# Matmuls of the K and V tiles as register-addressed loops, and a new split of the last weight rows

## The chip, the cores and the metric

The kernel runs on one core of one Trainium2 chip, in a single launch. The metric is device time in microseconds (us) of the whole program; the figure for a kernel is the median of its runs. Five engines work side by side and each runs its own instruction list in order: TensorE (PE in the profile; its weight loads are listed apart as PEld), VectorE (DVE), ScalarE (ACT), GpSimd (POOL) and SyncE (SP), which here only issues transfers. Transfers are carried out by 16 DMA engines. Engines and transfers wait for one another through semaphores.

## The reference, cut to what matters

One decode step: attention of one token over a cache of 65,536 keys and values for 8 heads of 256 (two query heads share each), a small gated feed-forward block, and a sigmoid gate that mixes the two.

```python
B, Sq, D = 1, 1, 448
Hq, Hkv, Sk, Dh = 16, 8, 65536, 256          # F = 1792, all bf16
g = _sigmoid((x * gate_w).sum(-1, keepdims=True))
# a:
q = (x @ wq).reshape(B, Sq, Hq, Dh).transpose(0, 2, 1, 3)
scores = jnp.einsum("bhqd,bhkd->bhqk", q, k) * (Dh ** -0.5)
o = jnp.einsum("bhqk,bhkd->bhqd", softmax(scores), v)
a = o.transpose(0, 2, 1, 3).reshape(B, Sq, Hq * Dh) @ wo
# b:
gate = x @ W_gate; up = x @ W_up
h = gate * (gate > 0) * up
b = h @ W_down
return g * a + (1 - g) * b
```

K and V are 268 MB each; all other inputs together are about 12 MB.

## The kernel before

**Tiles.** K and V are read in tiles of 16,384 positions of one head, each 128 partitions x 32768 bf16 (8.39 MB): 32 K tiles and 32 V tiles, four of each per head. They lie in a ring of three buffers, `ring[0]` to `ring[2]`. Every load of a tile goes out on SP's queue, in the order of the list `order`: the projection weights, K tiles 0 to 3, then V and K in turn, at the end V tiles 28 and 29, part of Wo, V tile 30, V tile 31 in three pieces and the rest of Wo. A load may be issued only when the matmuls that read the buffer's earlier tile are done (`free`, semaphore waits on SP). SP issues in order, so a load that waits holds back all behind it. `TILE = 19.35` is the time that the plan allows for a tile.

**K tile** (`kind == "k"`). VectorE transposes the tile in place in 32x32 blocks of 32-bit words (L379; the first four tiles in two halves, all others in one piece). Then TensorE computes scores (`f_qk`, 64 matmuls of 512 columns): the queries `xm` are the weights (16 columns), the transposed tile streams. Results go to two PSUM tiles `ST0` and `ST1`, each to four strips of 32 partitions. The strip is the matmul's `tile_position=(0, 32 * w)`, one of four column strips of TensorE's array that can work at the same time. The second matmul of a strip uses the weights that the first one loaded (`same_weights`, which leaves the weight load out). VectorE then joins the halves (L594) and takes the maximum (L596), ScalarE takes the exponential (L598). After the fourth K tile of a head a short chain over VectorE, TensorE and ScalarE scales the head's probabilities, which are then transposed (L604 to L624).

**V tile** (`make_pv`). TensorE multiplies probabilities `P0` or `P1` (32 weight columns) with the V tile, 128 matmuls of 512 columns to the four PSUM tiles `O0` to `O3` and four strips each. After a head's fourth V tile VectorE, TensorE and ScalarE collect the result (`o_copy`, `f_otr`, `f_nrm`). The last V tile comes in pieces, with small fill-in matmuls (`f_busy`) between them.

**Order.** The kernel lists operations with a key, the planned time (`op`, `dma`); `_Plan.finish` sorts each engine's operations by key and derives the semaphore waits; `emit` writes them out and lets the last instruction of each operation raise its engine's semaphore by one. The order on TensorE around a steady pair of tiles is: QK of a K tile, then PV of the V tile that has landed.

**Feed-forward rows.** 448 input rows are 3 x 128 + 64. The 64 rows left over of W_gate and W_up are loaded by `rows64` (L402 to L408) into `wfh`, in four transfers per matrix: 5 partitions with 4 rows each, again 5 with 4, 5 with 3, and 3 with 3, interleaved (partition `c + 4 i` of transfer `c`). `f_xp` (L307) lays the matching 64 entries of x out in the same pattern, and `f_gu2` (L556) multiplies them, over 20 partitions and four blocks; places without a row are zero.

Of the kernel before, what the change touches and what calls it, by code (L numbers as in the profile page):

```python
# [1 line left out]

# [13 lines left out]
class _Op:  # L16


    def __init__(self, eng, key, fn, deps, dma=None):
        self.eng, self.key, self.fn, self.dma = eng, key, fn, dma  # L20
        self.deps = [d for d in deps if d is not None]
        self.count = None


class _Plan:
# [8 lines left out]
    def op(self, eng, key, fn, deps=()):  # L34
        o = _Op(eng, key, fn, deps)
        self.ops.append(o)
        return o

# [14 lines left out]
    def finish(self):  # L53
        progs = {}
        for i, o in enumerate(self.ops):
            o.seq = i
            for d in o.deps:
                assert (d.key, d.seq if hasattr(d, "seq") else -1) <= (o.key, i), (o.eng, o.key, d.eng, d.key)
        for e in ("sp", "pe", "dv", "ac", "gp"):
            progs[e] = sorted((o for o in self.ops if o.eng == e), key=lambda o: (o.key, o.seq))  # L60
        ndma = {}
        for e, prog in progs.items():
            n = 0
            for o in prog:
# [12 lines left out]
        for o in sorted(self.ops, key=lambda o: (o.key, o.seq)):  # L77
            need, after = {}, {}
            for d in o.deps:
                k = ("d", d.dma) if d.dma is not None else ("e", d.eng)  # L80
                need[k] = max(need.get(k, 0), d.count)
                merge(after.setdefault(k, {}), d.known)
            o.waits = []
            for k, v in need.items():
                if past[o.eng].get(k, 0) < v and all(a.get(k, 0) < v for j, a in after.items() if j != k):
                    o.waits.append((k, v))
            merge(past[o.eng], need)
            for a in after.values():
                merge(past[o.eng], a)
            o.known = dict(past[o.eng])  # L90
        return progs
# [12 lines left out]
def bass_gated_mix__gqa_block_cached__glu_gated_reglu__decode_kernel(  # L104
# [23 lines left out]
    NT = H * NTH  # L128
# [11 lines left out]
    KR = D - NR3  # L140
# [3 lines left out]
    with es:  # L144
# [29 lines left out]
        xw = P2[0][:, 0:NW * 160]  # L174
# [132 lines left out]
        def f_xp(e):  # L307
            xr = x_row[0:1, NR3:D]
            for c in range(2):
                e.tensor_copy(x_per[0:1, 129 * c:129 * c + 127:2], xr)  # L310
            xp2 = x_per[0:1, 256:768].rearrange("o (b g p) -> o g b p", b=4, g=4)
            def two(v, b):
                return v.rearrange("o (i b) -> o b i", b=b).unsqueeze(1).to_broadcast([1, 2, b, v.shape[1] // b])
            for c in range(2):
                e.tensor_copy(xp2[:, 0:2, :, c:20:4], two(xr[:, 20 * c:20 * c + 20], 4))
            e.tensor_copy(xp2[:, 0:2, 0:3, 2:20:4], two(xr[:, 40:55], 3))
            return e.tensor_copy(xp2[:, 0:2, 0:3, 3:12:4], two(xr[:, 55:KR], 3))
        x0_ = op("dv", 0.5, f_xp, [d_x, c_xp])
        x1_ = mop("pe", 0.6, f_xT, [d_x, c_o1, x0_])

# [55 lines left out]
        def f_trans(sl, w, nw):  # L376
            m = U * DH // nw
            v = ring[sl][:, w * m:(w + 1) * m].bitcast(U32)
            return lambda e: e.transpose(v, v)  # L379

        def f_qk(n, sl):
            h = n // NTH
            kv = ring[sl][:].rearrange("p (u s c w j two) -> p s c w u j two", s=2, c=4, w=4, j=8, two=2)

            def f(e):
                for c in range(4):
                    for r_ in range(2):
                        x0 = ((h * 4 + c) * 2 + r_) * 16
                        for s_ in range(2):
                            for w in range(4):  # L390
                                o, v = ST[s_][32 * w:32 * w + 16, :], kv[:, s_, c, w, :, :, r_]
                                st = c == 0 and r_ == 0
                                if s_ == 0:
                                    ins = e.matmul(o, xm[:, x0:x0 + 16], v, start=st, stop=False, skip_group_check=True, tile_position=(0, 32 * w))  # L394
                                else:
                                    ins = same_weights(e, o, xm[:, x0:x0 + 16], v, st, (0, 32 * w))
# [76 lines left out]
        def make_pv(n, lo, hi, sl, tv, dep):  # L473
# [4 lines left out]
            def f_pv(e):  # L478
                for m in range(lo // 2, hi // 2):
                    I, i, g = m // 16, m // 4 % 4, m % 4  # L480
                    k = m if solo else I * 16 + g * 4 + i
                    b, n_ = (0, 4) if solo else (i, 32)
                    col = (k - b) * 32 + a
                    o, w = OP[b][32 * g:32 * g + n_, :], P2[h % 2][:, col:col + 4 * n_ - 3:4]
                    v = ring[sl][:, k * 512:(k + 1) * 512]
                    st = a == 0 and I == 0
                    if b == 0:
                        ins = e.matmul(o, w, v, start=st, stop=False, skip_group_check=True, tile_position=(0, 32 * g))  # L488
# [34 lines left out]
        for kind, i, t in issue:  # L523
# [59 lines left out]
            elif kind == "k":  # L583
# [10 lines left out]
                join = op("dv", tk + 25.2, lambda e: e.copy_predicated(  # L594
# [142 lines left out]
```

## Time and profile before

| | |
|---|---|
| median of 3 runs | 1277.44 us (1277.27 to 1277.6) |
| span of the profiled execution, first to last instruction | 1275.9 us |
| TensorE busy (matmul) | 353.7 us, 28% |
| VectorE busy | 683.4 us, 54% |
| ScalarE busy | 56.1 us, 4% |
| moved by DMA | 549.46 MB, mean 431 GB/s |

The profile is of one execution. Its span leaves out what lies around the program's first and last instruction, some 1.5 us against the median of the runs. A row of instructions gives the engine, the source line, the operation, what is written and read, the count, and, in brackets, how long the engine sat idle before it and whom it waited for. `SPq` rows are transfers being issued. Transfers have a time from issue to landing; what exceeds the pure transfer time was spent in the queue behind earlier ones. In a table of stretches each engine's busy time is followed by TensorE's granted clock (1.00 is full speed), the mean busy share of the 16 DMA engines, and GB/s.

### The profile page before, as it was taken

The numbers are of one execution on the slowest core, as the hardware profiler recorded it, in microseconds if no ns is written. First come the engines' busy times: TensorE is split into PE (matmuls) and PEld (weight loads), VectorE is DVE, ScalarE is ACT, GpSimd is POOL, SyncE is SP. The second block draws the span as 40 slices with busy tenths as digits, with TensorE's granted clock in tenths as the row PEclk, the third lists the DMA queues.
The fourth block names the chain that finished last, engine by engine and source line by source line (L and its number), as shares of the span: only waits on it lengthen the run. The fifth ranks groups of instructions, "written<-read, shape, count | busy, mean of one in ns | idle before, by whom it ended". The sixth has DMA issues, their size and how long they took to land.

```text
span 1275.9 us, 6860 instructions
## 1 busy us (share of the span) xinstructions
PE 353.7 (28%) x4446; PEld 71.6 (6%) x1875; DVE 683.4 (54%) x271; ACT 56.1 (4%) x104; POOL 10.6 (1%) x23
## 2 busy tenths in 40 slices
PE   3312323313122240133220242211323203322135
PEld 2000000000000000000000000000000000000010
DVE  2688733566534755445555454556535566336521
ACT  0000000000000000000000000000000000000000
POOL 3000000000000000000000000000000000000000
PEclk9566666665666565666755666656666556666577
DMA  9999999999999999999999999999999999999998
GB/s 407 433 436 434 438 428 429 442 427 436 431 426 448 429 428 434 430 434 438 428 434 438 430 434 428 432 438 438 428 428 436 436 438 428 428 438 436 434 417 372
DMA packets 11178, 549.46 MB, mean 431 GB/s; under 512 B 1255, under 2 KB 1386, under 8 KB 2154
## 3 DMA queue, kind: packets, MB, share of 16 engines
q1 hardware_dynamic: 11002, 547.66, 99.3%
q10 hardware_dynamic: 148, 1.38, 0.3%
q8 instruction: 24, 0.39, 0.1%
q14 instruction: 4, 0.03, 0.0%
HBM read 549.03 MB, written 0.00 MB: 430 GB/s over the span
## 4 chain that ended last, share of the span: by engine, by line
DVE 40%; DMA 28%; PE 17%; another core or an unknown queue 12%; ACT 1%; issue 1%; SPq 0%; ACTq 0%; DVEq 0%
DVE ring L379 32%; DMA ring<-in_A_k_cache_dram 24%; PE ST L394 5%; PE ST L420 5%; PE O L420 4%; DMA ring<-in_A_wo_dram 3%; DVE o_sb L429 2%; PE O L488 2%; DVE P L617 1%; DVE P L615 1%; ACT P L598 1%; DMA P<-in_A_x_dram 1%; DVE nmb L596 1%; DVE ST L594 1%
## 5 line engine op out<-in xcount | busy, mean ns | idle before, releaser
L379 DVE STREAM_TRANSPOSE ring<-ring 128x16384 uint32<-128x16384 uint32 (+1 forms) x36 | 552.3, 15345 | 315.9 <-DMA ring<-in_A_k_cache_dram 311.5
L394 PE MATMUL ST<-ring,xm 128*16 128x512 bf16 x1024 | 139.7, 537 | 769.2 <-DVE ring L379 769.2
L420 PE MATMUL ST<-ring,xm 128*16 128x512 bf16 x1024 | 136.7, 526 | 0.0
L420 PE MATMUL O<-ring,P 128*32 128x512 bf16 x1524 | 119.3, 425 | 0.0
L594 DVE COPY_PREDICATED ST<-bm,ST 128x512 f32<-128x512 uint16 x32 | 22.2, 693 | 169.3 <-PE ST L420 169.3
L598 ACT ACTIVATE P<-ST,nmb 128x512 bf16<-128x512 f32 x32 | 45.3, 1415 | 1099.3 <-DVE nmb L596 1099.3
L394 PEld LDWEIGHTS ST<-ring,xm 128*16 128x16 bf16 x1024 | 31.8, 115 | 925.8 <-DVE ring L379 797.9
L488 PE MATMUL O<-ring,P 128*32 128x512 bf16 (+1 forms) x524 | 56.7, 430 | 21.9 <-DMA ring<-in_A_v_cache_dram 21.9
L429 DVE CAST_PREDICATED o_sb<-bm,O 128x512 bf16<-128x512 uint16 (+1 forms) x33 | 22.3, 679 | 62.0 <-PE O L420 58.9
L615 DVE TENSOR_TENSOR P<-P,hs 128x2048 bf16<-128x2048 bf16 x8 | 18.3, 2292 | 8.7 <-ACT hs L612 8.7
L596 DVE TENSOR_REDUCE nmb<-ST 128x1 f32<-128x512 f32 x32 | 22.1, 691 | 1.1
L488 PEld LDWEIGHTS O<-ring,P 128*32 128x32 bf16 (+1 forms) x524 | 15.8, 114 | 119.3 <-issue 92.0
L617 DVE STREAM_TRANSPOSE P<-P 128x2048 bf16<-128x2048 bf16 x8 | 18.5, 2312 | 0.3
L622 PE MATMUL M_ps<-hs,ones_f 128*128 128x2 f32 x16 | 4.7, 363 | 46.0 <-DVE hs L621 46.0
L457 PE MATMUL M_ps<-emat,o_sb 128*64 128x2 bf16 x48 | 3.0, 184 | 22.1 <-ACT o_sb L439 22.1
L598 ACT ACTIVATION_READ_ACCUMULATOR P<-ST,nmb 128x1 f32 x32 | 8.5, 266 | 0.0
L345 PE MATMUL M_ps<-ring,P 128*128 128x256 bf16 x48 | 7.4, 330 | 0.3 <-DVE gb L297 0.3
L310 DVE COPY xm<-P 1x64 bf16<-1x64 bf16 x2 | 0.3, 189 | 11.9 <-DMA P<-in_A_x_dram 11.9
L622 PEld LDWEIGHTS M_ps<-hs,ones_f 128*128 128x128 f32 x16 | 4.0, 311 | 46.7 <-DVE hs L621 46.7
L608 PE MATMUL M_ps<-identf,hs 128*2 128x128 f32 x8 | 2.2, 277 | 15.7 <-DVE hs L606 15.7
L259 POOL MEMSET ring<- 64x7168 bf16 x1 | 6.1, 6064 | 0.3 <-POOLq L722 0.3
L345 PEld LDWEIGHTS M_ps<-ring,P 128*128 128x128 bf16 x48 | 5.6, 118 | 2.0 <-issue 0.4
(96 smaller groups left out, 82.6 us busy)
## 6 DMA issues: line engine op xcount, KB each, us to landing
ring<-in_A_v_cache_dram SPq DMA_DIRECT2D x1, 4096.0 KB, 29.6
ring<-in_A_v_cache_dram SPq DMA_DIRECT2D x2, 2048.0 KB, 36.0
ring<-in_A_wq_dram SPq DMA_DIRECT2D x1, 3072.0 KB, 13.3
ring<-in_A_wo_dram SPq DMA_DIRECT2D x1, 1792.0 KB, 19.4
ring<-in_B_W_down_dram SPq DMA_DIRECT2D x1, 1568.0 KB, 17.2
ring<-in_B_W_gate_dram ACTq DMA_DIRECT2D x1, 1344.0 KB, 13.1
ring<-in_B_W_up_dram SPq DMA_DIRECT2D x1, 1344.0 KB, 15.9
ring<-in_A_wo_dram SPq DMA_DIRECT2D x1, 896.0 KB, 40.0
```

Source lines behind the costliest of these rows:

```text
L345: ins = e.matmul(QN_ps, xw3[:, kt, 31 - j:159 - j], wq3[:, kt * NQ + j * 256:kt * NQ + (j + 1) * 256], start=(j == 0 and kt == 0), stop=Fa ...
L379: return lambda e: e.transpose(v, v)
L394: ins = e.matmul(o, xm[:, x0:x0 + 16], v, start=st, stop=False, skip_group_check=True, tile_position=(0, 32 * w))
L420: return e.add_instruction(mybir.InstMatmult(name=nc.get_next_instruction_name(), engine=e.engine, ins=[e.lower_ap(v), e.lower_ap(w, for_m ...
L429: return e.copy_predicated(dst, m.to_broadcast(list(src.shape)), src)
L488: ins = e.matmul(o, w, v, start=st, stop=False, skip_group_check=True, tile_position=(0, 32 * g))
L594: join = op("dv", tk + 25.2, lambda e: e.copy_predicated(ST[0][:], bm[:, NB:NB + 1].bitcast(mybir.dt.uint16).to_broadcast([128, 512]), ST[ ...
L596: smax[n] = op("dv", tk + 26, lambda e, n=n, NM=NM, t_=t_: e.tensor_reduce(NM[:, t_:t_ + 1], ST[0][:], AX.X, ALU.max, negate=True), [join, ...
L598: aexp[n] = op("ac", tk + 27, lambda e, n=n, t_=t_, NM=NM, RS=RS, Ph=Ph: e.activation(Ph[:, t_:2048:4], ST[0][:], ACTF.Exp, bias=NM[:, t_: ...
L615: rsc = op("dv", T + 16, lambda e, X=X, pb=pb: e.tensor_tensor(pb, pb, X[:, 12:16].unsqueeze(1).to_broadcast([128, 512, 4]), ALU.mult), [h ...
L617: last["ev", h] = [op("dv", T + 17, lambda e, Ph=Ph: e.transpose(Ph[:], Ph[:]), [rsc])]
L622: l3 = mop("pe", T + 19, lambda e, X=X: e.matmul(LS_ps, ones_f[:, :], X[:, 6:8], start=True, stop=True), [l2, c_one])
```

## The change

Two edits.

1. **Loops on TensorE.** `f_qk` writes out its first eight matmuls and then runs the other 56 as a loop of seven passes with eight matmuls. `f_pv` does the same for the V tiles 0 to 30 with 16 matmuls a pass: three passes after 16 written-out matmuls for a head's first V tile, four passes and nothing written out for the others. The last V tile stays as it was. Weight and data addresses are computed from the loop counter in TensorE's registers (`moved`, `raw_mm`). The last matmul of each pass raises the semaphore, so an operation now counts 7, 4 or 3 (`incs`). Inside a QK pass, and among the eight written out, the two matmuls that share a strip now follow each other.

2. **The 64 rows.** The four transfers per matrix now take 5 partitions with 4 rows three times, and 4 partitions with one row; `f_xp` follows.

```diff
@@ _Op, _Plan
-                    n += 1
+                    n += o.incs
@@ f_xp
-            for c in range(2):
+            for c in range(3):
                 e.tensor_copy(xp2[:, 0:2, :, c:20:4], two(xr[:, 20 * c:20 * c + 20], 4))
-            e.tensor_copy(xp2[:, 0:2, 0:3, 2:20:4], two(xr[:, 40:55], 3))
-            return e.tensor_copy(xp2[:, 0:2, 0:3, 3:12:4], two(xr[:, 55:KR], 3))
+            return e.tensor_copy(xp2[:, 0:2, 0:1, 3:16:4], two(xr[:, 60:KR], 1))
@@ f_qk
+        def moved(ap, by):
+            return dataclasses.replace(ap, offset=ap.offset + by)
+
+        def raw_mm(e, o, w, v, pos, load):
+            return e.add_instruction(mybir.InstMatmult(
+                name=nc.get_next_instruction_name(), engine=e.engine, ins=[v, w], outs=[e.lower_ap(o)],
+                start_tensor_calc=False, stop_tensor_calc=False, tile_size=(128, 32), tile_position=pos,
+                bass_skip_group_check=True, ldweights=None if load else False))
...
-                for c in range(4):
-                    for r_ in range(2):
-                        x0 = ((h * 4 + c) * 2 + r_) * 16
+                x0 = h * 8 * 16
+                for w in range(4):
+                    for s_ in range(2):
+                        o, v = ST[s_][32 * w:32 * w + 16, :], kv[:, s_, 0, w, :, :, 0]
+                        if s_ == 0:
+                            e.matmul(o, xm[:, x0:x0 + 16], v, start=True, stop=False, skip_group_check=True, tile_position=(0, 32 * w))
+                        else:
+                            same_weights(e, o, xm[:, x0:x0 + 16], v, True, (0, 32 * w))
+                with e.Fori(1, 8, 1) as k:
+                    by = (k >> 1) * 64 + (k & 1)
+                    xw = e.lower_ap(moved(xm[:, x0:x0 + 16], k * 16), for_matmul_weights=True)
+                    vs = [[e.lower_ap(moved(kv[:, s_, 0, w, :, :, 0], by)) for s_ in range(2)] for w in range(4)]
+                    for w in range(4):
                         for s_ in range(2):
-                            for w in range(4):
...
+                            ins = raw_mm(e, ST[s_][32 * w:32 * w + 16, :], xw, vs[w][s_], (0, 32 * w), s_ == 0)
@@ rows64
-            for c, (n, m, r0) in enumerate(((5, 4, 0), (5, 4, 20), (5, 3, 40), (3, 3, 55))):
+            for c, (n, m, r0) in enumerate(((5, 4, 0), (5, 4, 20), (5, 4, 40), (4, 1, 60))):
@@ make_pv
+            def f_pv_loop(e):
+                with e.Fori(0 if a else 1, 4, 1) as I:
+                    ws = [e.lower_ap(moved(P2[h % 2][:, g * 128 + a:g * 128 + a + 125:4], I * 512), for_matmul_weights=True) for g in range(4)]
+                    vs = [[e.lower_ap(moved(ring[sl][:, (g * 4 + i) * 512:(g * 4 + i + 1) * 512], I * 8192)) for i in range(4)] for g in range(4)]
+                    for i in range(4):
+                        for g in range(4):
+                            ins = raw_mm(e, OP[i][32 * g:32 * g + 32, :], ws[g], vs[g][i], (0, 32 * g), i == 0)
                 return ins
+            looped = n < NT - 1
+            if looped and a:
+                f_pv = f_pv_loop
...
-            pv[n] = op("pe", tp, f_pv, deps)
+            pv[n] = op("pe", tp, f_pv, deps, incs=(4 if a else 3) if looped else 1)
@@ K tile
-                qk[n] = op("pe", tk + 18, f_qk(n, sl), [tr[-1], l_["xm"], c_ps[1]])
+                qk[n] = op("pe", tk + 18, f_qk(n, sl), [tr[-1], l_["xm"], c_ps[1]], incs=7)
```

The order of instructions on TensorE at the last K tile (31), before: the last eight of its 64 scores matmuls (the 56 ahead of them read the same), the three of the head's closing chain, and the beginning of PV of V tile 28. A row is the source line, the operation, what is written and read, its size, and a count of equal neighbours; `x4` here are four different strips.

```order
L394 MATMUL ST0<-ring2,xm 16x512 x4
L420 MATMUL ST1<-ring2,xm 16x512 x4
L608 MATMUL M_ps<-identf,hs1 2x128
L610 MATMUL M_ps<-mx2,nselT 128x1
L622 MATMUL M_ps<-hs1,ones_f 128x2
L488 MATMUL O0<-ring0,P1 32x512 x4
L420 MATMUL O1<-ring0,P1 32x512 x4
L420 MATMUL O2<-ring0,P1 32x512 x4
```

The same K tile in the changed kernel, from the last strip of the eight written-out matmuls through the head of the loop to the second strip of a pass:

```order
L400 MATMUL ST0<-ring2,xm 16x512
L433 MATMUL ST1<-ring2,xm 16x512
L403 UNCONDITIONAL_BRANCH
L403 ISA
L406 REGISTER_ALU x2
L406 ISA x4
L385 MATMUL ST0<-ring2,xm 16x512
L385 MATMUL ST1<-ring2,xm 16x512
L385 MATMUL ST0<-ring2,xm 16x512
```

What moved: `ST0` and `ST1` of one strip now alternate, and each of the seven passes begins with seven register steps (`ISA` is a fused group of up to six register operations) and ends with an increment and a branch.

PV of V tile 28 in the changed kernel, on TensorE behind the scores of K tile 31, from the first group of the 16 written-out matmuls' end to the loop's branch:

```order
L433 MATMUL O3<-ring0,P1 32x512 x4
L511 UNCONDITIONAL_BRANCH
L511 ISA
L512 ISA x2
L513 ISA x7
L513 REGISTER_ALU
L385 MATMUL O0<-ring0,P1 32x512 x4
L385 MATMUL O1<-ring0,P1 32x512 x4
L385 MATMUL O2<-ring0,P1 32x512 x4
L385 MATMUL O3<-ring0,P1 32x512 x4
L511 REGISTER_ALU
L511 COMPARE_AND_BRANCH
```

What moved: the order of the matmuls over tiles and strips is the same as before; eleven register steps stand ahead of the 16 matmuls of each pass, an increment and a branch behind them. Across the program TensorE's matmul instructions go from 4,430 to 1,534 written, in 63 loops.

More of the change, by code (lines that the diff above doesn't have):

```diff
@@ L1 @@
+import dataclasses
 from contextlib import ExitStack
@@ L16, with __init__ @@
 class _Op:
-    def __init__(self, eng, key, fn, deps, dma=None):
-        self.eng, self.key, self.fn, self.dma = eng, key, fn, dma
+    def __init__(self, eng, key, fn, deps, dma=None, incs=1):
+        self.eng, self.key, self.fn, self.dma, self.incs = eng, key, fn, dma, incs
         self.deps = [d for d in deps if d is not None]
@@ L32, in __init__, with op @@
         self.dsem = {}
-    def op(self, eng, key, fn, deps=()):
-        o = _Op(eng, key, fn, deps)
+    def op(self, eng, key, fn, deps=(), incs=1):
+        o = _Op(eng, key, fn, deps, incs=incs)
         self.ops.append(o)
@@ L490, in f_pv @@
                         ins = same_weights(e, o, w, v, st, (0, 32 * g))
-                return ins
+                    if looped and m == 15:
+                        break
+                if not looped:
+                    return ins
+                return f_pv_loop(e)
+            def f_pv_loop(e):
[5 more added lines that the diff above has]
+                            ins = raw_mm(e, OP[i][32 * g:32 * g + 32, :], ws[g], vs[g][i], (0, 32 * g), i == 0)
+                return ins
+            looped = n < NT - 1
+            if looped and a:
+                f_pv = f_pv_loop
             tp = max(tv, last["tev", h])
             deps = [dep] + last["ev", h] + ([last.get(("ocp", h - 1)), l_["hT"]] if a == 0 else [])
-            pv[n] = op("pe", tp, f_pv, deps)
+            pv[n] = op("pe", tp, f_pv, deps, incs=(4 if a else 3) if looped else 1)
             if n == NT - 1 and lo == PIECES[1][0]:
```

6 lines of the change are left out of this document (removed).

## The prediction

> **What bounds the kernel now.** First the page: span, busy engines, DMA.
>
> ```profile
> span 1275.9 us, 6860 instructions
> ...
> PE 353.7 (28%) x4446; PEld 71.6 (6%) x1875; DVE 683.4 (54%) x271; ACT 56.1 (4%) x104; POOL 10.6 (1%) x23
> ...
> DMA packets 11178, 549.46 MB, mean 431 GB/s; under 512 B 1255, under 2 KB 1386, under 8 KB 2154
> ...
> q1 hardware_dynamic: 11002, 547.66, 99.3%
> ...
> q8 instruction: 24, 0.39, 0.1%
> ```
>
> No compute engine is over 54%, and the data queue keeps the 16 DMA engines busy for 99.3% of the span: 549.46 MB at 431 GB/s is the whole 1275 us. A ring tile is 128 x 32768 bf16, 8.39 MB, so 8.39 MB / 431 GB/s = 19.5 us. Compute can cost time only where it hands back a ring buffer so late that a DMA engine runs dry. So the second thing to read is how early each transfer is issued: the time from issue to landing of the V loads from 200 to 1175 us, then of the K loads there, then of the V load issued at 130.25, last of the V load issued at 1226.05 (tile 30).
>
> ```profile
> DMA to landing us min/median/max: 34.3/34.9/51.4
> ...
> DMA to landing us min/median/max: 38.9/50.8/52.0
> ...
> DMA to landing us min/median/max: 30.9/30.9/30.9
> ...
> DMA to landing us min/median/max: 24.0/24.0/24.0
> ```
>
> What exceeds 19.5 us is time in which the queue was still working on earlier tiles, the slack of that issue: 14.8 us at least for V and 19.4 us at least for K in the middle, 11.4 us for V tile 1, and 4.5 us for V tile 30. Who hands the buffers back is in the DMA queue's own waits:
>
> ```profile
> SPq L634 <- PE ST L420: 902.0, 29, 36.3
> SPq L587 <- PE O L420: 165.4, 27, 15.5
> ```
>
> V loads (L634) wait for the QK matmuls, K loads (L587) for the PV matmuls: exactly the two pieces of code that become loops. Third, the thinnest place, from the last K tile to the issue of V tile 30:
>
> ```profile
> 1205.01 0.61 PE L394 MATMUL ST<-ring,xm 128*16 128x512 bf16 x4 [26.53 <-DVE ring L379]
> 1205.40 0.64 PE L420 MATMUL ST<-ring,xm 128*16 128x512 bf16 x4
> ...
> 1210.10 0.55 PE L394 MATMUL ST<-ring,xm 128*16 128x512 bf16 x4
> 1210.48 0.38 PE L420 MATMUL ST<-ring,xm 128*16 128x512 bf16 x4
> 1210.69 0.38 PE L394 MATMUL ST<-ring,xm 128*16 128x512 bf16 x4
> ...
> 1220.75 0.63 PE L488 MATMUL O<-ring,P 128*32 128x512 bf16 x4
> ...
> 1224.11 0.39 PE L488 MATMUL O<-ring,P 128*32 128x512 bf16 x4
> ...
> 1225.19 0.82 PE L420 MATMUL O<-ring,P 128*32 128x512 bf16 x12
> ...
> 1226.05 0.34 SPq L634 DMA_DIRECT2D ring<-in_A_v_cache_dram  x1
> ...
> 1274.75 0.28 SPq L698 DMA_DIRECT2D out_dram<-P  x1
> ...
> 1225.00:1226.00 1.00, 1.00 (x20) 0.00 (x0) 0.00 (x0) 0.00 (x0) 0.00 (x0) 1.00 0.64 265
> 1226.00:1227.00 1.00, 0.55 (x16) 0.12 (x4) 0.00 (x0) 0.00 (x0) 0.00 (x0) 1.00 0.80 337
> ```
>
> The two last rows are 1 us stretches; their last columns are granted clock, DMA share, GB/s. QK of tile 31 takes 1205.01 to 1211.3, 6.3 us: four matmuls every 0.43 us until 1210.1, then every 0.21. PV of tile 28 takes 1220.75 to 1226.05, 5.3 us, slow until about 1224. Then V tile 30 is issued, and a third of the DMA engines has already run dry (share 0.64). This is the place that has no cover left. From the 4.5 us goes the way from issue to first data; the output, issued at 1274.75 with the span's end at 1275.9, bounds it at 1.1 us. So a later issue is free for at most 3.4 us, and for 0 if the dry engines are those that end last. The share says that two thirds still work then, and the dry ones have finished first throughout: I take **2.0 us**.
>
> **The change, part by part.** (1) *QK order.* Eight matmuls per pass were ordered so that each group of four went to four different 32-column strips of the array; now the two that share a strip stand next to each other. A 512-column matmul occupies its strip for 0.43 us slow, 0.21 fast (the starts above, four at a time). If a waiting matmul holds up those behind it, strips work two at a time: a pass takes 4 x 0.43 = 1.72 us slow or 0.86 fast instead of half; if it does not, nothing changes. No row has two matmuls of four strips in such an order, so these are the bounds, and I take the first. [...]
>
> (2) *Loop control.* A QK pass adds 9 instructions (5 fused register steps, 1 or 2 plain ones, increment, branch) to 8 matmuls and 4 weight loads; a PV pass adds 13 to 16 and 4. None is in the trace of before. The nearest rows:
>
> ```profile
> 14.71 0.15 PEld L302 LDWEIGHTS M_ps<-one_t,P 1*128 1x128 bf16 x3 [14.71 <-DVE xm L317]
> 14.79 0.23 PEld L304 LDWEIGHTS M_ps<-one_t,xm 1*128 1x128 bf16 x6
> 14.82 0.29 PE L304 MATMUL M_ps<-one_t,xm 1*128 1x1 bf16 x6
> ```
>
> Nine pairs, 18 tiny instructions, go through from 14.71 to 15.11: 22 ns each, the floor. The ceiling is SP's DMA issue above, 0.34 us. Between ends that far apart I take their geometric mean, 0.09 us. A QK pass then needs 12 x 0.022 + 9 x 0.09 = 1.07 us of issuing, a PV pass 20 x 0.022 + 13 x 0.09 = 1.61 us. Issuing can run beside the matmuls of the pass ahead, so the larger of issue and array counts.
>
> QK of tile 31: the first eight 5 x 0.43 = 2.15 us, slow passes until 5.1 us (1.7 of them), then 5.3 passes. At 0.86 (issue ran ahead) the end is at 9.7 us, at 1.07 (it did not) at 10.8; I take 10.2, **+3.9 us**. PV of tile 28: the order over strips stays; 16 matmuls outside the loop 1.7 us, then three passes, against 3.2 us of slow clock: 5.8 us with the issue running ahead, 6.9 without, against 5.3: +0.5 to +1.6, I take **+1.1 us**. V tile 30 is issued 5.0 us later; less 2.0 of slack, **+3.0 us**. What is late next are V 30, the three V pieces and the last Wo rows, one queue; nothing after them has cover.
>
> (3) *Elsewhere hidden.* In the middle a V issue is late by 3.9 against 14.8, a K issue by 5.0 against 19.4: nothing. At the beginning the K tiles come one after another, and DVE's next step waits for QK as soon as it is longer than the half transpose beside it:
>
> ```profile
> 96.01 17.31 DVE L379 STREAM_TRANSPOSE ring<-ring 128x8192 uint32<-128x8192 uint32 x2 [1.46 <-ACT P L598]
> 113.24 0.67 DVE L594 COPY_PREDICATED ST<-bm,ST 128x512 f32<-128x512 uint16 x1
> ...
> 130.26 0.70 DVE L594 COPY_PREDICATED ST<-bm,ST 128x512 f32<-128x512 uint16 x1 [5.45 <-PE ST L420]
> ```
>
> Half a transpose is 17.31 / 2 = 8.7 us, QK of tile 3 is 5.4. With 10.2 us, tiles 1 and 2 push DVE by 1.5 each, and V tile 1 is issued 4.8 + 3.0 = 7.8 us later, against 11.4: hidden. If the cover were gone it would cost those 7.8.
>
> (4) *Rows of W_gate and W_up.*
>
> ```profile
> ring<-in_B_W_gate_dram SPq DMA_DIRECT2D x2, 70.0 KB
> ring<-in_B_W_up_dram SPq DMA_DIRECT2D x2, 70.0 KB
> ring<-in_B_W_gate_dram SPq DMA_DIRECT2D x1, 52.5 KB
> ...
> ring<-in_B_W_gate_dram SPq DMA_DIRECT2D x1, 31.5 KB
> ```
>
> One partition is one engine's piece: 14 KB, 10.5 KB. At 431 / 16 = 27 GB/s that is 0.53 and 0.40 us. If the same lowest engines take each of these loads, the busiest had 4 x 0.53 + 4 x 0.40 = 3.7 us for both matrices and gets 6 x 0.53 + 2 x 0.13 = 3.4: a gain of at most 0.3 us, none where the queue runs dry at the end anyway: 0. (5) *Instruction loads.* PE's program halves, so of 24 instruction packets about 12 go, 0.2 MB or 0.5 us of the queue's rate, with the same end: 0.
>
> **Sum.** 1275.9 + 3.0 = 1278.9 us in the profiled execution. The median of the runs is 1277.44, 1.5 above that span, so 1277.44 + 3.0 = **1280.4 us**.
>
> **Rivals.** *A, hidden (not slower).* Strips don't hold each other up, or the slack at the end is near 3.4: what is left of the 5.0 us is covered or costs 1 at most, and the rows and the halved instruction loads give back up to 0.8: 1276.6 to 1278.4. For it: PE is busy 28% of the span, and every place but one has over 11 us of slack. Against it: that one place.
>
> *B, dear control.* It decides from QK of 11.4 us on, where (X - 5.4) + 2 (X - 8.7) exceeds the 11.4 of V tile 1. At 0.15 us per control instruction a QK pass is 1.61 us, QK 12.0, PV 8.1: the start loses 1.8, the end 5.7 + 2.8 - 2.0 = 6.5: 1285.7. At 0.3 us QK is 21.5 and PV 13.6: 30 at the start and 21 at the end: 1329. For it: each fused step holds six register operations. Against: the floor is 22 ns.
>
> *C, loops that lie across two instruction blocks.* 24 packets of 0.39 MB for 6321 PE instructions are blocks of 16 KB, one per 256 instructions. Some 3,100 instructions in 63 loops of about 21 or 33 leave five to nine loops across a border. If each return fetches the block just left,
>
> ```profile
> q1 hardware_dynamic: 13, 0.85, 133.1%
> q8 instruction: 1, 0.02, 4.6%
> ```
>
> (a stretch of 1.5 us with one such packet: 4.6% of 16 x 1.5 = 1.1 us), it waits 1.1 us and up to one 64 KB row before it (19.5 / 8 = 2.4 us). Six returns of 3.5 are 21 us in a QK loop, 3.9 more with the order, against 14.8: 10 us for each; two of them: 1300. In a PV loop 2 or 3 returns stay under 19.4. For it: one packet comes for each block of instructions, so blocks are replaced all the time. Against: nothing shows that it is the block just left that goes. [...]
>
> *D, faster by more than 0.2%.* It would need more than the 0.8 us above.
>
> **How the numbers follow.** A measurement of this kernel can tell about 0.2%, 2.55 us, from no change: 1274.9 to 1280.0. Forecast 38% (1278.5 to 1283, some two fifths of it under 1280.0), A 19%, B 20%, C 20%, D 3%. Same: 19 + 15 = 34%; slower: 23 + 20 + 20 = 63%; faster 3%. The range runs from 1277 (the upper part of A) to 1308 (B to 0.2 us per control instruction, C with two loops); beyond it lie a part of A, D, and the far ends of B and C, under 2 in 10.
>
> **What would show it.** QK of tile 31 near 10 us with starts in twos; PV of tile 28 near 6.4; the V load of tile 30 issued about 1231, with a stretch of DMA share near zero before it; V tile 1 issued about 138 without a gap after it. B shows as QK over 11.4 and a gap near 137 us; C as more than 24 instruction packets and single loops of over 20 us; A as an issue before 1228. A QK under 8 us or over 12 makes the sum wrong, and so does any gap in the middle.

## The result, and the profile after

The changed kernel takes 1282.29 us (median of 5 runs, 1281.42 to 1282.64) against 1277.44 us for the kernel before (5 runs): ratio 1.0036, 95% interval 1.0025 to 1.0047, **4.85 us slower**; forecast were +3.0 and 1280.4. Set on the chip once more beside other kernels it took 1281.18 us (7 runs, 1280.47 to 1281.57), ratio 1.0030 (1.0019 to 1.0041), +3.8 us. The profiled execution of the first set, used below, is its slowest: 1282.64 us with a span of 1281.2.

First the page of the changed kernel: span, engines, DMA, queues.

```profile
span 1281.2 us, 10420 instructions
...
PE 485.3 (38%) x4447; PEld 69.4 (5%) x1875; DVE 683.5 (53%) x271; ACT 55.7 (4%) x104; POOL 10.6 (1%) x23
...
DMA packets 11170, 549.26 MB, mean 429 GB/s; under 512 B 1257, under 2 KB 1388, under 8 KB 2164
...
q1 hardware_dynamic: 11006, 547.66, 99.0%
...
q8 instruction: 12, 0.20, 0.1%
```

PE does the same matmuls in 485 us of busy time in place of 354; the data queue's share falls from 99.3 to 99.0% over a longer span. Twelve instruction packets, half of before.

Then the time from issue to landing, in the order of the prediction: V loads from 200 to 1175 us, K loads there, V tile 1 (issued at 136.43), V tile 30 (issued at 1232.29).

```profile
DMA to landing us min/median/max: 30.5/30.7/31.7
...
DMA to landing us min/median/max: 34.4/42.5/43.6
...
DMA to landing us min/median/max: 25.9/25.9/25.9
...
DMA to landing us min/median/max: 23.0/23.0/23.0
```

The middle keeps 30.5 - 19.5 = 11.0 us of slack for V and 14.9 for K: at the least, loads have 3.8 and 4.5 us less than before (34.3 - 30.5, 38.9 - 34.4), the median K load 8.3 us less (50.8 - 42.5), and nothing comes of it. The end has none left, which the timeline from QK of tile 31 to the issue of V tile 30 shows (last bracket: idle before, and its releaser):

```profile
1206.19 0.61 PE L400 MATMUL ST<-ring,xm 128*16 128x512 bf16 x4 [17.81 <-DVE ring L379]
1206.58 0.65 PE L433 MATMUL ST<-ring,xm 128*16 128x512 bf16 x4
1207.22 1.04 PE L385 MATMUL ST<-ring,xm 128*16 x8
1208.51 1.03 PE L385 MATMUL ST<-ring,xm 128*16 x8 [0.25 <-issue]
...
1215.09 1.03 PE L385 MATMUL ST<-ring,xm 128*16 x8 [0.25 <-issue]
1216.18 0.39 SPq L688 DMA_DIRECT2D ring<-in_A_wo_dram  x1
...
1225.70 0.62 PE L501 MATMUL O<-ring,P 128*32 128x512 bf16 x4
...
1226.11 1.49 PE L433 MATMUL O<-ring,P 128*32 128x512 bf16 x12
...
1227.39 5.79 PE L385 MATMUL O<-ring,P 128*32 x60
...
1232.29 0.33 SPq L663 DMA_DIRECT2D ring<-in_A_v_cache_dram  x1
```

QK takes 1206.19 to 1216.18, 10.0 us (6.3 before), PV of tile 28 1225.70 to 1232.29, 6.6 us (5.3 before). Between the QK passes PE stands idle for 0.25 us and more with nothing to wait for but its own issuing. In PV of tile 28 no row has idle time before it (the row of 60 runs on into the next tile). A V tile takes 64 matmuls of 512 columns, here 16 and three passes of 16; the 128 in the description of the kernel before are too many. The stretches around the issue, whose last columns are granted clock, DMA share and GB/s:

```profile
1226.00:1228.00 2.00, 2.00 (x24) 0.16 (x4) 0.55 (x2) 0.00 (x0) 0.00 (x0) 0.50 0.97 401
1228.00:1230.00 2.00, 2.00 (x28) 0.16 (x4) 0.00 (x0) 0.00 (x0) 0.00 (x0) 0.50 0.37 154
1230.00:1232.00 2.00, 2.00 (x28) 0.15 (x4) 0.00 (x0) 0.00 (x0) 0.00 (x0) 0.59 0.04 18
```

From 1230 to 1232 us the DMA engines move 18 GB/s: they have run dry, all of them. That is where the time went. The transfer of a tile reports sixteen completions, read here as one for each DMA engine; those of V tile 30 came from 1247.58 to 1250.08 before and come from 1253.60 to 1255.32 now: 5.24 us later for the last, of a span longer by 5.3.

What a pass waits for stands in the trace's records of PE's sequencer, which the rows above leave out. One QK pass of tile 31 (start in us, duration in us, operation):

```
1211.206 0.036 ALU_OP            (increment)
1211.302 0.213 COMPARE_BRANCH
1211.573 0.100 FUSED_REGOPS
1211.731 0.036 ALU_OP
1211.828 0.036 ALU_OP
1211.925 0.083 FUSED_REGOPS
1212.066 0.080 FUSED_REGOPS
1212.205 0.080 FUSED_REGOPS
1212.343 0.074 FUSED_REGOPS
1212.467 0.088 LDWEIGHTS         (first of four, the last at 1212.487)
1212.496 0.036 ALU_OP            (the next increment)
```

Nine control instructions take 1212.467 - 1211.206 = 1.26 us, 0.14 each; four weight loads and the issue of eight matmuls take the 0.03 that is left. From one fused step to the next are 0.133 us (median of 1792 pairs in the run), from the branch to what follows it 0.27 (269 pairs).

### The profile page after: what moved, and what is told of

Read it like the earlier page. It is cut to its first block, busy times and chain, and to the rows that moved or that the text cites. A ratio compares the mean times of both kernels' runs of the same rounds, so it can differ in the third digit from the quotient of the medians.

```text
span 1281.2 us, 10420 instructions
## 1 busy us (share of the span) xinstructions
PE 485.3 (38%) x4447; PEld 69.4 (5%) x1875; DVE 683.5 (53%) x271; ACT 55.7 (4%) x104; POOL 10.6 (1%) x23
## 4 chain that ended last, share of the span: by engine, by line
DMA 49%; DVE 27%; PE 20%; issue 4%; ACT 1%; SPq 0%; ACTq 0%
DMA ring<-in_A_k_cache_dram 45%; DVE ring L379 22%; PE ST L385 9%; PE O L385 6%; DMA ring<-in_A_wo_dram 3%; DVE P L646 1%; DVE P L644 1%; DMA P<-in_A_x_dram 1%; PE ST L400 1%; PE O L433 1%; PE M_ps L345 1%; DVE nmb L625 1%; DVE ST L623 1%; PE ST L433 1%; PE M_ps L639 0%
## 5 line engine op out<-in xcount | busy, mean ns | idle before, releaser
L385 PE MATMUL ST<-ring,xm 128*16 x1792 | 229.1, 604 | 52.8 <-issue 51.2
L400 PE MATMUL ST<-ring,xm 128*16 128x512 bf16 x128 | 19.5, 594 | 553.3 <-DVE ring L379 553.3
L385 PE MATMUL O<-ring,P 128*32 x1856 | 166.9, 501 | 56.2 <-issue 55.6
L385 PEld LDWEIGHTS ST<-ring,xm 128*16 x896 | 24.1, 87 | 258.8 <-issue 258.8
L400 PEld LDWEIGHTS ST<-ring,xm 128*16 128x16 bf16 x128 | 3.3, 87 | 576.9 <-DVE ring L379 576.9
L385 PEld LDWEIGHTS O<-ring,P 128*32 x464 | 14.9, 112 | 210.7 <-issue 210.7
L433 PE MATMUL ST<-ring,xm 128*16 128x512 bf16 x128 | 20.6, 629 | 0.0
L433 PE MATMUL O<-ring,P 128*32 128x512 bf16 x132 | 14.4, 563 | 0.0
L501 PE MATMUL O<-ring,P 128*32 128x512 bf16 (+1 forms) x60 | 7.2, 507 | 3.6 <-DMA ring<-in_A_v_cache_dram 3.4
```

The lines of the kernel that those rows point to most:

```text
L385: return e.add_instruction(mybir.InstMatmult(name=nc.get_next_instruction_name(), engine=e.engine, ins=[v, w], outs=[e.lower_ap(o)], start ...
L400: e.matmul(o, xm[:, x0:x0 + 16], v, start=True, stop=False, skip_group_check=True, tile_position=(0, 32 * w))
L433: return e.add_instruction(mybir.InstMatmult(name=nc.get_next_instruction_name(), engine=e.engine, ins=[e.lower_ap(v), e.lower_ap(w, for_m ...
```

## The experiments

**Theory after this profile**: the loops' control instructions pace QK and PV, and that costs only where the last K tile and V tile 28 hand back the buffers for V tile 30. **Rivals**: the strip order inside the QK loop does it; the new row split does it; the loops cost elsewhere too. "Written out" means the code of the kernel before for that tile (`f_out`); `NT` is 32. All times below are medians, with the ratio to the kernel before on the same chip (1277.39 to 1277.44 us each time) and its 95% interval.

**1. The rows alone.**

```diff
-            for c, (n, m, r0) in enumerate(((5, 4, 0), (5, 4, 20), (5, 3, 40), (3, 3, 55))):
+            for c, (n, m, r0) in enumerate(((5, 4, 0), (5, 4, 20), (5, 4, 40), (4, 1, 60))):
```

(against the kernel before; `f_xp` follows)

> Only the new split of the last 64 rows (six pieces of four rows where there were four and four of three); K and V matmuls all written out in the old order. Theory (loop control in two places makes the loss): the V load of tile 30 is issued at 1226.0 +- 0.3 us as before, QK of tile 31 takes 6.3 us, and the span is 1275.9 us within 0.8. Rival (the row split is what delays the queue from the start): W_down lands last at about 45.8 us in place of 45.06, everything after it is 0.8 to 1.2 later, span 1276.7 to 1277.1.

1277.67 us, ratio 1.0003 (0.9994 to 1.0013); V tile 30 issued at 1225.61, span 1276.4. W_down lands last at 45.56, between the two expectations, but nothing that can be measured follows. The rows are not the loss.

**2. The two places at the end written out.** To the changed kernel:

```diff
-            return f
...
+            return f if qk_looped(n) else f_out
+
+        def qk_looped(n):
+            return n != NT - 1
...
-            looped = n < NT - 1
+            looped = n < NT - 1 and n != NT - 4
```

> The changed kernel with QK of tile 31 and PV of tile 28 written out in the old order; all other tiles loop. Theory (the end has no cover): QK of tile 31 back to 6.3 us, PV of tile 28 to 5.3, the V load of tile 30 issued 1.2 us after that of before (1227.3), span 1275.9 + 1.2 = 1277.1, time about 1278.6. Rival (the loops cost in the middle, or by the queue's rate): the span stays at 1280 or more.

1277.67 us, ratio 1.0001 (0.9992 to 1.0010): the whole loss is gone, although 31 QK and 30 PV blocks still loop. Timeline of this kernel at the place:

```profile
1205.62 0.61 PE L403 MATMUL ST<-ring,xm 128*16 128x512 bf16 x4 [17.72 <-DVE ring L379]
...
1211.99 0.39 SPq L703 DMA_DIRECT2D ring<-in_A_wo_dram  x1
...
1226.74 0.34 SPq L678 DMA_DIRECT2D ring<-in_A_v_cache_dram  x1
```

**3. Only these two places as loops**, all else as in the kernel before:

```diff
-            return f
...
+            return f if qk_looped(n) else f_out
+
+        def qk_looped(n):
+            return n == NT - 1
...
-            looped = n < NT - 1
+            looped = n == NT - 4
```

(lines against the changed kernel; the old row split comes back with them)

> The kernel before with its old row split, only QK of tile 31 and PV of tile 28 as loops. Theory: QK of tile 31 takes 10.0 us, PV of tile 28 6.5, the V load of tile 30 is issued about 1231.0, and the span is 1275.9 + 4.1 = 1280.0, time about 1281.4. Rival (the two loops at the end are covered): 1277.5 within 0.8.

1281.26 us, ratio 1.0031 (1.0020 to 1.0042), span 1279.9, V tile 30 issued at 1230.78. Two loops out of 63 make the loss of all 63.

**4. The first five QK written out** in the changed kernel:

```diff
-            return f
...
+            return f if qk_looped(n) else f_out
+
+        def qk_looped(n):
+            return n > 4
```

> The changed kernel with QK of tiles 0 to 4 written out in the old order; all else loops. Theory: the V load of tile 1 goes out at 130.5 us in place of 136.4, the first engines no longer run dry there, and some 0.4 us come back: time about 1281.9. Rival (the start makes the whole shift of 1.2 us that the last K tile showed): 1281.1. If the start matters not at all: 1282.3.

V tile 1 goes out at 131.77 us in place of 136.43. 1281.53 us, ratio 1.0032 (1.0020 to 1.0044): inside what the changed kernel's two sets span (1281.18 and 1282.29). Whether the start costs the 0.4 us that was expected can't be told.

**5. Strips apart in the loop**, the old order with the new control:

```diff
-                    for w in range(4):
-                        for s_ in range(2):
+                    for s_ in range(2):
+                        for w in range(4):
```

(and the same for the eight matmuls ahead of the loop)

> The changed kernel with the old order of strips in the QK loop and in the eight matmuls ahead of it: four matmuls for four different strips, then four more. Theory (a pass is paced by its nine control instructions, the strip order costs nothing): QK of tile 31 takes 10.0 us with passes 1.29 to 1.33 us apart, time 1282.3 within 0.8. Rival (pairs that share a strip hold up the others, as the prediction had it): QK of tile 31 falls to 8 us or less, time about 2 us lower, 1280.3.

QK of tile 31 takes 9.7 us (1205.58 to 1215.28), with passes again 1.29 to 1.33 us apart. 1281.16 us, ratio 1.0029 (1.0019 to 1.0040). This is 1.1 us under the first set of the changed kernel, 0.0 under the second (experiment 12), so nothing of it shows as the order's.

**6. Strips together without a loop**: all QK written out, in the new order.

```diff
-                        for s_ in range(2):
-                            for w in range(4):
+                        for w in range(4):
+                            for s_ in range(2):
```

(in the code of the kernel before; PV loops)

> All QK matmuls written out, but in the new order (the two that share a strip next to each other); PV loops and rows as in the changed kernel. Theory (the array takes matmuls of other strips past a waiting one, as far as the starts in fours show): QK of tile 31 takes 6.3 us as before, PV of tile 28 6.5, so the V load of tile 30 is 1.2 to 1.8 us later than before (1227.3 to 1227.9), and with 0.7 of that covered the time is 1278.4 within 0.8. Rival (strict program order, strips work two at a time): passes of 1.72 us slow and 0.86 fast, QK of tile 31 10 us or more, time 1281 or more.

1277.63 us, ratio 1.0001 (0.9992 to 1.0010). Its timeline at tile 31:

```profile
1205.45 0.61 PE L403 MATMUL ST<-ring,xm 128*16 128x512 bf16 x4 [23.89 <-DVE ring L379]
1205.85 0.64 PE L448 MATMUL ST<-ring,xm 128*16 128x512 bf16 x4
1206.27 0.64 PE L403 MATMUL ST<-ring,xm 128*16 128x512 bf16 x4
1206.70 0.64 PE L448 MATMUL ST<-ring,xm 128*16 128x512 bf16 x4
...
1210.57 0.39 SPq L703 DMA_DIRECT2D ring<-in_A_wo_dram  x1
```

The program now alternates L403 and L448 (first and second half of a strip's pair), yet the trace has four starts of L403, then four of L448, 0.43 us apart, exactly as with the old order. QK takes 5.1 us. Here a matmul that waited for its strip did not hold up those behind it that went to other strips. Had it done so, QK would have taken over 8 us by the prediction's passes, an estimate (1.7 slow passes of 1.72 in the 3.0 us before the clock rose, 6.3 of 0.86 after it). The time is 0.8 under what was expected, since V tile 30 went out at 1226.24: the clock rose earlier in QK, and PV of tile 28 took 6.4 us.

**7. One loop, QK of tile 31**, all else as in the kernel before.

```diff
-            return f
...
+            return f if qk_looped(n) else f_out
+
+        def qk_looped(n):
+            return n == NT - 1
...
-            looped = n < NT - 1
+            looped = False
```

(lines against the changed kernel; the old row split comes back with them)

> The kernel before with only QK of tile 31 as a loop. Theory: QK of tile 31 10.0 us in place of 6.3, the V load of tile 30 issued 3.7 later (1229.8). With the 0.7 us of cover that the run with both loops showed: time 1277.4 + 3.0 = 1280.4. If the prediction's cover of 2.0 holds: 1279.1. If cover is 2.7 or more (the last engine's lead): 1278.4.

1280.99 us, ratio 1.0029 (1.0017 to 1.0040), span 1278.9; V tile 30 issued at 1230.09, 4.04 us later than before. One loop carries nearly the whole loss, and the cover is 4.04 - 3.0 = 1.0 us, not 2.0. Its timeline settles what paces a pass:

```profile
1209.05 1.03 PE L386 MATMUL ST<-ring,xm 128*16 x8 [0.32 <-issue]
1210.34 1.02 PE L386 MATMUL ST<-ring,xm 128*16 x8 [0.26 <-issue]
1211.68 0.61 PE L386 MATMUL ST<-ring,xm 128*16 x8 [0.32 <-issue]
1213.01 0.61 PE L386 MATMUL ST<-ring,xm 128*16 x8 [0.72 <-issue]
1214.30 0.77 PE L386 MATMUL ST<-ring,xm 128*16 x8 [0.68 <-issue]
```

From the pass at 1211.68 on TensorE has the fast clock (granted 0.50 from 1204 to 1211 us, 0.74 in the mean from 1211 to 1218), and the matmuls of a pass shrink from 1.03 to 0.61 us, but passes stay 1.29 to 1.34 us apart; the idle time takes up the difference. The array did not set the pace of this loop.

**8. Two QK steps in a pass**: sixteen matmuls written out, then three passes of sixteen.

```diff
-                with e.Fori(1, 8, 1) as k:
-                    by = (k >> 1) * 64 + (k & 1)
...
+                with e.Fori(1, 4, 1) as c:
+                    xw = [e.lower_ap(moved(xm[:, x0 + 16 * r_:x0 + 16 * r_ + 16], c * 32), for_matmul_weights=True) for r_ in range(2)]
+                    vs = [[[e.lower_ap(moved(kv[:, s_, 0, w, :, :, r_], c * 64)) for s_ in range(2)] for w in range(4)] for r_ in range(2)]
...
```

> The changed kernel with two QK steps in a pass: sixteen matmuls written out, then three passes of sixteen with ten fused register steps, increment and branch each. Theory (cost goes by control instructions: 0.13 us for a fused step, 0.3 for the branch with its refill): a pass takes 1.75 us, about what its matmuls take at the slow clock (four by 0.43), so QK of tile 31 takes 7.3 us, the V load of tile 30 goes out 2.7 us earlier than in the changed kernel, and the time is about 1279.6. Rival (a loop costs by its matmuls with addresses in registers, not by its control): QK of tile 31 stays at 10 us, time 1282.3.

1277.72 us, ratio 1.0001 (0.9992 to 1.0010). QK of tile 31 takes 6.4 us as if written out:

```profile
1205.49 0.61 PE L402 MATMUL ST<-ring,xm 128*16 128x512 bf16 x4 [21.67 <-DVE ring L379]
...
1207.16 4.66 PE L385 MATMUL ST<-ring,xm 128*16 x48
1211.87 0.39 SPq L690 DMA_DIRECT2D ring<-in_A_wo_dram  x1
...
1226.08 1.06 PE L385 MATMUL O<-ring,P 128*32 x16 [0.59 <-issue]
```

There is no idle time between the QK passes. The expected 7.3 us was too careful: control of a pass (1.85 to 1.9 us from its first fused step to the next pass's) runs beside the sixteen matmuls ahead of it, which take 4 x 0.43 = 1.7 us, so hardly anything sticks out. All 63 loops are still there, PV of tile 28 among them, with 15 instruction packets in place of 24, at no cost that the time shows. PV of tile 28 took 5.9 us with 0.59 us of idle time ahead of its last pass, and V tile 30 went out at 1227.17, 1.1 later than in the kernel before.

**9 to 11. Another layout of the 64 rows.** In the kernel before the last engine's completion of W_down comes 4.1 us after the first, and of the last K tile 4.9. Each small row transfer has only five or three pieces, one for a partition. If the same few engines carry all of these and that lag sets the end, sixteen pieces should help. To the kernel before (9), and to the kernel of experiment 8 with PV of tile 28 written out (10):

```diff
-            for c, (n, m, r0) in enumerate(((5, 4, 0), (5, 4, 20), (5, 3, 40), (3, 3, 55))):
...
+            d_ = dma("sp", t, sem, lambda e: e.dma_start(
+                wfh[32 * i_:32 * i_ + 16, :], W[NR3:D, :].rearrange("(i b) f -> i (b f)", b=4)), [z_f])
```

(`f_xp` follows)

> The kernel before with the last 64 rows of W_gate and W_up on sixteen partitions of four rows, and nothing else changed. Theory: the small transfers put 1.1 us on every engine in place of 3.7 on five, so the lag at W_down falls from 4.1 to under 3; 24 instruction packets of 1.1 us each still fall on some engines during the run, so less is left of it at the end than with loops: time 1276.8 within 0.6. Rival (the lag has another cause): 1277.4.

> Loops with two QK steps in a pass, PV of tile 28 written out, and the last 64 rows of W_gate and W_up laid on sixteen partitions of four rows, one transfer each, in place of four transfers on five. Theory (the end is set by the engine that lags most from the start, 4.1 to 4.8 us at W_down, because the same few engines carry all the small row transfers): the spread of W_down's landing falls from 4.7 us to under 3, the V load of tile 30 is issued at about 1226.5 and lands last within 1 to 1.5 us of its first piece, about 1249.3 in place of 1250.6, and the time is about 1276.3, 1 us under the kernel before. Rival (the lag has another cause, or sixteen pieces land on few engines as well): spread stays over 4, time 1277.5.

Both miss: 1282.50 us, ratio 1.0041 (1.0027 to 1.0054), and 1280.37, ratio 1.0023 (1.0013 to 1.0032). The lag did fall (W_down from 46.24 to 47.17 in the first of them), but everything came later, and more so as it went on: in experiment 9 by 2.1 us at W_down and by 5.3 at K tile 31 (1192.97 against 1187.69); where the further 3.2 us arise is open. Stretches of the kernel of experiment 9 in which the two transfers run:

```profile
36.00:38.00 2.00, 0.00 (x0) 0.00 (x0) 0.00 (x0) 0.00 (x0) 0.00 (x0) 0.50 1.16 165
38.00:40.00 2.00, 0.00 (x0) 0.00 (x0) 0.50 (x1) 0.00 (x0) 0.00 (x0) 0.50 0.84 90
40.00:42.00 2.00, 0.00 (x0) 0.00 (x0) 2.00 (x1) 0.00 (x0) 0.00 (x0) 0.50 0.91 113
```

The DMA engines are busy and move 90 to 165 GB/s. The 32 pieces of 14336 bytes took 1.75 us each in the mean (0.54 to 2.17) where they took 0.54 in the kernel before. Experiment 11, otherwise the kernel of experiment 10, moves them apart, W_gate to partitions 0, 8, ..., 120 and W_up to 4, 12, ..., 124 (`f_xp` and `f_gu2` follow, and the zeros are written to all 128 partitions):

```diff
-                wfh[32 * i_:32 * i_ + 16, :], ...
+                wfh[4 * i_:4 * i_ + 121:8, :], ...
```

> As the run with sixteen partitions, two QK steps in a pass and PV of tile 28 written out, but the sixteen pieces of W_gate lie on partitions 0, 8, ..., 120 and those of W_up on 4, 12, ..., 124, the weights of x moved to match. Theory (sixteen pieces at once into sixteen neighbouring partitions took 1.0 to 2.2 us each in place of 0.54, and that cost the 3 to 4 us; spread out they take 0.54 each, 1.1 us on every engine): W_down lands from about 42 to 43.5 us, with less than 2.5 us between first and last, the V load of tile 30 is issued at about 1226, lands last at about 1248.8, and the time is about 1275.9, 1.5 us under the kernel before. Rival (one transfer of sixteen pieces is slow wherever it lands): pieces of 1.5 us or more again, time 1280 or more.

1278.43 us, ratio 1.0008 (0.9999 to 1.0017). The pieces took 0.88 us in the mean (0.54 to 1.06), and W_down's last completion comes 1.3 us before that of the kernel before (43.79 against 45.06). But by K tile 1 this lead is gone (64.37 against 64.42), after an instruction packet of 1.07 us at 45.44, and at K tile 31 it is a lag of 0.9 (1188.59 against 1187.69); V tile 30 goes out at 1228.02, since PV of tile 28, written out, had the slow clock until 1227.2 and took 6.4 us. The expectation fell. That instruction packets now fall on the engines that end last was argued, not shown. None of these versions beats the kernel before.

**12. The changed kernel again.**

> The changed kernel once more, beside the two above. If the 1.1 us between it and the run with the old strip order in the loop came from the order, it is at 1282.3 again; if it is the scatter of kernels whose engines all run dry (which engine an instruction packet falls on, and the clock that the QK and PV loops happen to get), it comes out between 1281.1 and 1282.3.

1281.18 us, ratio 1.0030 (1.0019 to 1.0041): the order was not it. Here QK of tile 31 took 9.6 us, PV of tile 28 5.9 and V tile 30 went out at 1230.23. Of the stretch 1226 to 1232 us the granted clock was 0.82 here and 0.53 in the first profile:

```profile
1226.00:1232.00 6.00, 5.10 (x68) 0.42 (x12) 0.00 (x0) 0.00 (x0) 0.00 (x0) 0.82 0.80 297
```

```profile
1226.00:1232.00 6.00, 6.00 (x64) 0.46 (x12) 0.55 (x2) 0.00 (x0) 0.00 (x0) 0.53 0.46 191
```

(This kernel first, then the first profile of the changed one.) Once V tile 30 waits for PE, the clock of those microseconds enters the time: that is a source of the wider scatter, 1280.5 to 1282.6 over both sets against 1277.1 to 1278.4 for the kernel before.

## Why the prediction was right, and where not

**The bound and the place.** Right. The lateness of V tile 30 and what it costs, in us, over the kernels that touch the place:

| kernel | V tile 30 issued | later than before | its completions, first to last | span | longer than before |
|---|---|---|---|---|---|
| before | 1226.05 | | 1247.58 to 1250.08 | 1275.9 | |
| changed, first profile | 1232.29 | 6.2 | 1253.60 to 1255.32 | 1281.2 | 5.3 |
| changed, second | 1230.23 | 4.2 | 1251.44 to 1253.31 | 1279.2 | 3.3 |
| 3: two loops only | 1230.78 | 4.7 | 1252.09 to 1252.99 | 1279.9 | 4.0 |
| 7: one loop only | 1230.09 | 4.0 | 1251.52 to 1252.34 | 1278.9 | 3.0 |
| 2: end written out | 1226.74 | 0.7 | 1248.30 to 1250.69 | 1276.5 | 0.6 |
| 8: two steps a pass | 1227.17 | 1.1 | 1248.43 to 1250.61 | 1276.4 | 0.5 |

**(1) QK order: wrong.** It was taken as strips working two at a time, 1.72 us a pass slow and 0.86 fast. Experiments 5 and 6 show no cost; of the two bounds the other held. The announced starts in twos never came; they come in fours. No run shows the two strips at a time that these passes stand for: in the same order without a loop (experiment 6) eight matmuls took 0.85 us slow and 0.43 fast. Without the order the prediction's own control figure still gives a QK term: 0.26 us of issuing, seven passes of 1.07 and the last matmuls' 0.43 are 8.2 us, +1.9.

**(2) Loop control: the mechanism right, its size too small.** 0.09 us for a control instruction measured 0.14; the 0.022 for each load and matmul measured 0.03 us for all twelve. A QK pass of tile 31 needs 1.31 us of issuing (1.33 is the median of the run from branch to branch) in place of 1.07, a PV pass 1.88 (median from branch to branch) in place of 1.61. So QK of tile 31 came out at 10.0 and 9.6 us, against 10.2 forecast, by a sum with two faults that offset each other: a wait of the array that no run shows, and control dearer by half (0.14 for 0.09), a pass by a quarter (1.31 for 1.07). That the sum came out is luck. Forecast were passes of 0.86 or 1.07 us at the fast clock and 1.72 at the slow; measured is 1.31 at the slow clock and 1.29 to 1.34 at the fast (experiment 7).

**PV of tile 28: near by luck too.** Forecast was 6.4, measured are 6.6 and 5.9. In the first profile PE has no idle time in it and the granted clock is 0.50 to 1230 us: the slow clock, not control, makes that 6.6. Over all runs this PV took 5.1 to 6.4 us written out and 5.9 to 6.6 looped, by when the clock rose. Where it rose 2.9 to 3.0 us after the beginning, PV took 5.1 written out (experiment 1) and 5.9 looped (8); where it rose after 5.6 to 5.7, 6.4 both ways (11 and 6). So the loop itself adds from nothing to 0.8 us here, and in the first profile the 1.3 is the clock's. What decides when the clock rises is open.

**The 2.0 us of cover: too large.** The last two columns give 0.7 to 1.0. One reason is the way from issue to data, put at no more than 1.1 us from the output transfer. In the profile before, the engines that had run dry completed V tile 30 21.5 us after its issue (1226.05 to 1247.58), and in the changed kernel the first engine needed 21.3, where consecutive tiles complete 19.36 us apart: the way is 2.0 to 2.2. The last engine was busy until 1230.72 with the Wo rows, 4.7 us past the issue. That leaves 4.7 - 2.1 = 2.6 of cover, and the last completion of V tile 30 did move by less than the issue, by 1.0 in both profiles of the changed kernel and by 1.8 in experiments 3 and 7. The rest went after it. With all engines dry, each later delay of one engine counts: an instruction packet of about 1 us lies in the trace at 1243.8 in the changed kernel, and at 1266.7 and 1258.4 in experiments 3 and 7. The kernel before has one at 1253.8 as well, which cost it nothing that shows; that it fell on an engine with time to spare fits, but which engine took a packet was inferred only.

**The sum.** Forecast: 5.0 late less 2.0. First profile: QK +3.7, PV +1.3, 0.1 between them and 1.2 by which QK of tile 31 began later (1206.19 against 1205.01), less 0.9: 5.3. Second: 3.3 + 0.6 + 0.1 + 0.2, less 0.9: 3.3. The late beginning was no term of the forecast. It varies (0.2 to 1.2), and experiments 1 and 4 did not tie it to the rows or to the start.

**(3) Elsewhere hidden: right.** Experiment 2 is the proof: with only the end written out the loss is gone. V tile 1 was issued at 136.43 us (forecast about 138). K loads lost more than the 5.0 us forecast, 8.3 in the median: over the run a tile's QK takes 9.9 us where it took 5.8, and its PV 6.7 where it took 3.6 (medians). The slack of 19.4 covered it.

**(4), (5) Rows and instruction loads at nothing: right** within what can be measured; packets fell from 24 to 12 as forecast.

**Rivals.** A (hidden) falls with an issue at 1232.29 and 1230.23 in place of one before 1228; one of its conditions, strips that don't hold each other up, came true, but control alone made QK late. B (dear control) put its threshold at QK of 11.4 us; control is nearly as dear as it supposed (0.14 against 0.15), but the twelve cheap instructions of a pass keep QK at 10. C (loops across two instruction blocks) falls with 12 packets: the loops fetched no block again, and the V issues of the middle all keep 30.5 to 31.7 us to landing, which a QK loop of over 20 us would not leave. D (faster) falls with the time.

## What to carry to other kernels

In this kernel a loop on TensorE's sequencer cost its control instructions, one after the other: 1.26 us a pass, for a body whose matmuls took as little as 0.61. So count them per pass and put enough work into it to cover them: with twice the matmuls in a pass (experiment 8) the time was that of the kernel before, ratio 1.0001. Where transfers have slack, loop freely, and write out or widen only the one or two bodies whose end releases a transfer that nothing covers. A total that comes out right is no proof of its terms: only kernels that changed one term at a time showed that the strip order was free.

## What the runs showed of the hardware

- In the trace of the changed kernel fused register steps are 0.133 us apart (median of 1792 pairs), plain ones 0.10 (204 pairs), and the fused step after a loop's branch comes 0.27 us after it (269 pairs), while four weight loads and eight matmuls go out in 0.03 us.
- PE's matmuls for a free 32-column strip passed one that waited for a busy strip (experiment 6: starts in fours, 0.43 us apart, from a program that alternates).
- Sixteen pieces of one transfer that went to sixteen neighbouring partitions (experiment 9) took 1.75 us in the mean and up to 2.17 for 14336 bytes, in place of 0.54 for the kernel before's pieces of that size; all engines together moved 90 and 113 GB/s from 38 to 42 us. Spread by eight partitions (experiment 11) they took 0.88 in the mean and up to 1.06. Why the partitions matter no run shows.
